# A delta-rule attention and feed-forward kernel: halves of the inverse by pairs, turns in transpose mode, one more block by quarters, and an opening written out step by step

## The chip, the core and the metric

The kernel runs on one core of one Trainium2 chip. A core has a matrix engine (PE), whose weight loads (PEld) overlap its matmuls, a vector engine (DVE), a scalar engine (ACT), a third engine for simple work on SBUF (POOL), and an engine (SP) that here only issues transfers. Each runs its own list of instructions strictly in order, and they wait for each other through semaphores. PE writes to PSUM, and DVE or ACT must copy the result from there to SBUF before PE can use it again. The metric is the device time of one execution in microseconds (us), median of several; less is better.

## What is computed

```python
k_n = k / (norm(k, axis=-1) + 1e-6)
state = zeros(B, H, D, D)                       # B=4, H=8, S=768, D=48
for t in range(S):
    y[t]  = q[t] @ state
    v_old = k_n[t] @ state
    state = state + beta[t] * outer(k_n[t], v[t] - v_old)
x = y.transpose(0, 2, 1, 3).reshape(B * S, H * D)          # 3072 x 384
h = x @ w_in                                               # 384 x 2048
out = maximum(0.01 * h, h) @ w_out                         # 2048 x 384
```

All of it is in float32.

## The kernel before

**Tiling.** The 768 steps are cut into 12 blocks `n` of 64. Inside a block the recurrence becomes matrix algebra: the triangular matrix made of the products of keys and of `beta` has to be inverted for each of the 32 heads and sequences, and the state is then carried from block to block. The 32 are cut into two groups `g` of 16. The feed-forward part treats the 256 rows of a block in 16 units `f`: `first` (L522) makes 9 matmuls into `ph`, ACT and DVE split the result into a high and a low part (`gh`, `gl`), and `second` (L537) makes 6 matmuls into `po`. Products that have to be exact are thus made of three products of such parts; the small ones of the attention use plain float32, which shows as two records per matmul.

**The steps of a block.** A letter stands for each, with the block and group it works on:

- `Q` loads k and q, `G` (gram, L173) multiplies them into `pg`, and ACT copies the part for the inverse to `gs`; `O` (L194) writes it to DRAM as `gd`, `I` (L225) reads it back as `L` with one matrix per partition; `R` (L203) masks the other part for later use; `M` (L217) copies corners that the halves need.
- `e` advances the inverse on DVE by one step (`inverse`, L294): norms, set-up, then one elimination per column. Blocks 0 and 1 are inverted together, by quarters of 16 rows: 15 eliminations give the diagonal blocks of 16 x 16. Every other block takes 31 eliminations on halves of 32 x 32.
- `D` (L327) writes the inverse to DRAM as `td`, `t`/`T` (L339) a turned copy as `tt`, and `A` (L352) reads both back, heads on the free axis, into `rt` and `gm`.
- For blocks 0 and 1, `P`, `H`, `J` (`halves_a`, `_b`, `_c`, L370 to L404) join quarters to halves on PE: `P` turns one quarter and multiplies the corner by another, `H` multiplies the two, `J` turns the result. One product is made per head and half: 64, 32 and 16 matmuls per group. For later blocks `C` (L406) moves the copy that came through DRAM.
- `Z` and `U` (L414, L426) join the two halves; `F`, `N` bring the norms, `V` scales v; `K`, `W`, `S`, `Y` (L470 to L504) are the products with keys, values, state and queries; `X` (`columns`, L506) turns y into `x` by a matmul with the identity, one per 128 columns and group, and splits it into `xh` and `xl`.
- `B` loads k, v and q of a block for these products; `c` loads beta.

The weights arrive as raw words (`l`, L115), and `w` takes them through 7 steps of conversion on ACT and DVE in turn (`convert`, L119), 16 tiles of 768 KB. Until block 0's units are done these conversions run beside them.

**What sets the order.** The program is emitted in a written order, and every engine keeps it. `PROLOGUE` is a text of such letters that ends with `X@0`; then for each block and unit a small plan (`PLAN` for blocks 0 to 3, `STEADY` for the rest) names what is emitted before and after the unit's `first` and `second`. `second` runs two units behind. A step is emitted whole: its matmuls and, right behind them, the copies that ACT or DVE make of the result. While block n is in the feed-forward part, the attention of block n+1 and the inverse of n+2 are interleaved with it. Transfers are issued from SP, and the first ones also from ACT (`kq` of blocks 0 and 1, the first two weight tiles). Four PSUM banks rotate among the small products.

## Time and profile before

| | us |
|---|---|
| median of 3 runs (lowest, highest) | 680.76 (677.38, 685.29) |
| the profiled execution's own time | 679.8 |
| its span | 678.0 |
| busy: PE, DVE, ACT, POOL | 614.3, 443.0, 350.9, 6.5 |
| bytes moved, mean rate | 60.48 MB, 89 GB/s |
| ph, 1728 matmuls, first one at | 76.2 |

The page gives busy times of engines, slices of the span, the chain of work that ended last, and groups of equal instructions. A row of the chain reads: start, length, engine (or "issue", where the engine waited for nothing that the profile shows), output tile, source line and number of records. A row of a group reads: line, engine, operation, output<-inputs, shapes, count, then busy us, mean ns of one, idle time before it and what ended that.

### The profile page before, as it was taken

What the parts mean: (1) busy time and instruction counts of PE and PEld (TensorE: products, weight loads), DVE (VectorE), ACT (ScalarE), POOL (GpSimd) and SP (SyncE); (2) the same over time, 40 slices, a digit from 0 to 9 for tenths busy, and PEclk for the clock granted to TensorE, in tenths of its full rate; (3) what the DMA queues carried; (4) which work ended last, traced back from release to release, by engine and by line L of the source; (5) the groups of instructions that cost most, each with busy time, mean ns of one, the idle gap of its engine ahead of it and who ended that gap; (6) DMA issues with size and microseconds to landing.
All of it is one profiled execution on the core that took longest, in us unless ns stands there. A gap on an engine that the chain in (4) does not pass through costs nothing.

```text
span 678.0 us, 22510 instructions
## 1 busy us (share of the span) xinstructions
PE 614.3 (91%) x9192; PEld 582.7 (86%) x9192; DVE 443.0 (65%) x1957; ACT 350.9 (52%) x875; POOL 6.5 (1%) x12
## 2 busy tenths in 40 slices
PE   4026878999999998999999999999999999999997
PEld 3025767989898898999999999999999999999996
DVE  4895759688868766777667578578577676621221
ACT  3544647734654654646556545555545546465432
POOL 3000000000000000000000000000000000000000
PEclk9999968999999999999999999999999999999999
DMA  8884562343235235247056064154353360340001
GB/s 207 202 266 165 117 207 48 77 82 63 65 82 100 57 86 104 51 88 148 3 110 128 7 133 99 43 102 94 70 90 80 80 104 10 72 71 3 16 10 23
DMA packets 126279, 60.48 MB, mean 89 GB/s; under 512 B 112992, under 2 KB 116192, under 8 KB 126176
## 3 DMA queue, kind: packets, MB, share of 16 engines
q1 hardware_dynamic: 125488, 56.57, 38.5%
q10 hardware_dynamic: 688, 2.48, 1.3%
q8 instruction: 72, 1.18, 0.7%
q14 instruction: 31, 0.25, 0.1%
HBM read 46.70 MB, written 12.32 MB: 87 GB/s over the span
## 4 chain that ended last, share of the span: by engine, by line
PE 74%; DVE 11%; DMA 6%; issue 3%; ACT 2%; SPq 2%; ACTq 0%; DVEq 0%
PE ph L528 28%; PE po L545 24%; PE pk L474 3%; PE py L502 3%; PE pw L482 3%; PE pg L188 2%; PE pc L492 2%; PE px L513 2%; PE pu L432 2%; PE pz L422 2%; DMA kq<-in_kqT 2%; DVE tmp L266 2%; DVE T L271 1%; DMA wr<-in_w_all 1%; DMA L<-gd 1%
## 5 line engine op out<-in xcount | busy, mean ns | idle before, releaser
L528 PE MATMUL ph<-xh,w 128*128 128x256 f32 x1152 | 248.0, 291 | 3.0 <-DVE gl L534 2.9
L528 PEld LDWEIGHTS ph<-xh,w 128*128 128x128 f32 x1152 | 192.6, 191 | 11.9 <-DVE gl L534 5.2
L534 DVE TENSOR_TENSOR gl<-ph,gh 128x256 fp32r<-128x256 f32 x192 | 81.2, 423 | 183.3 <-ACT ph L533 181.5
L545 PE MATMUL po<-w,gh 128*128 128x384 f32 x768 | 198.4, 340 | 0.3 <-ACT ob L551 0.3
L528 PE MATMUL ph<-xl,w 128*128 128x256 f32 x576 | 163.2, 283 | 0.0
L532 ACT ACTIVATE gh<-ph 128x256 fp32r<-128x256 f32 x192 | 74.0, 385 | 159.4 <-PE ph L528 144.4
L545 PEld LDWEIGHTS po<-w,gh 128*128 128x128 f32 x768 | 129.9, 190 | 0.5 <-ACT ob L551 0.5
L545 PE MATMUL po<-w,gl 128*128 128x384 f32 x384 | 130.0, 339 | 0.0
L528 PEld LDWEIGHTS ph<-xl,w 128*128 128x128 f32 x576 | 110.1, 191 | 0.0
L271 DVE TENSOR_TENSOR T<-T,tmp 128x60 f32<-128x60 f32 (+4 forms) x600 | 98.3, 204 | 0.7
L266 DVE TENSOR_TENSOR tmp<-T,L 128x60 f32<-128x60 f32 (+4 forms) x600 | 97.6, 203 | 0.4
L533 ACT ACTIVATE ph<-ph 128x256 f32<-128x256 f32 x192 | 72.8, 379 | 0.0
L545 PEld LDWEIGHTS po<-w,gl 128*128 128x128 f32 x384 | 72.8, 190 | 0.0
L210 DVE TENSOR_TENSOR rq<-pg,csb 64x256 f32<-64x256 f32 x92 | 38.9, 423 | 7.5 <-ACT gs L192 5.8
L188 PE MATMUL pg<-kq 48*64 48x128 f32 x736 | 28.8, 295 | 7.4 <-DMA kq<-in_kqT 7.3
L476 ACT ACTIVATE rt<-pk 48x512 f32<-48x512 f32 x44 | 26.1, 593 | 16.9 <-PE pk L474 16.1
L188 PEld LDWEIGHTS pg<-kq 48*64 48x64 f32 x736 | 22.5, 144 | 12.2 <-DMA kq<-in_kqT 6.6
L484 ACT COPY rv<-pw 64x384 f32<-64x384 f32 x46 | 21.8, 473 | 14.8 <-PE pw L482 13.9
L482 PEld LDWEIGHTS pw<-rv,rt 128*64 128x64 f32 x768 | 24.6, 143 | 2.8 <-ACT gh L532 2.5
L192 ACT COPY gs<-pg 128x256 f32<-128x256 f32 x46 | 15.0, 382 | 22.9 <-PE pg L188 22.9
L474 PEld LDWEIGHTS pk<-rt,rk 64*48 64x48 f32 x704 | 22.0, 126 | 5.1 <-ACT ph L533 2.8
L502 PEld LDWEIGHTS py<-rv,rq 128*64 128x64 f32 x768 | 23.7, 138 | 2.9 <-ACT ph L533 2.5
(80 smaller groups left out, 616.1 us busy)
## 6 DMA issues: line engine op xcount, KB each, us to landing
wr<-in_w_all SPq DMA_DIRECT2D x14, 768.0 KB, 10.0
kq<-in_kqT SPq DMA_DIRECT2D x44, 192.0 KB, 4.4
L<-gd SPq DMA_DIRECT2D x22, 256.0 KB, 3.8
rk<-in_kv SPq DMA_DIRECT2D x24, 192.0 KB, 4.1
rv<-in_kv SPq DMA_DIRECT2D x24, 192.0 KB, 4.4
rq<-in_qT SPq DMA_DIRECT2D x24, 192.0 KB, 4.7
out<-ob SPq DMA_DIRECT2D x48, 96.0 KB, 2.2
gd<-gs SPq DMA_DIRECT2D x96, 32.0 KB, 1.7
```

What stands on the lines that cost most here:

```text
L188: nc.tensor.matmul(pt[b][c * 64:(c + 1) * 64, p * 128:(p + 1) * 128], kq[r, c ^ b, p, 0], kq[r, c ^ b, p].rearrange("p x t -> p (x t)"), s ...
L210: nc.vector.tensor_tensor(qa[DN, c, b * NPAIR:(b + 1) * NPAIR], pv[b][r, 1], tri[r].rearrange("p (o t) -> p o t", o=1).broadcast_to([C, NP ...
L266: nc.vector.tensor_tensor(tv, t[:, :, j:j + 1].broadcast_to([P, k, w]), L[:, j, j + 1:].rearrange("p (o w) -> p o w", o=1).broadcast_to([P ...
L271: nc.vector.tensor_tensor(t, t, tv, ALU.subtract)
L474: nc.tensor.matmul(pv[r, u], k[DN, c, u], t[DN, c, u], start=True, stop=True)
L482: nc.tensor.matmul(pv[r, u], t[:, c, u], v[:, c, u], start=True, stop=True)
L502: nc.tensor.matmul(pv[s * C:(s + 1) * C, u * D:(u + 1) * D], qa[:, c, u], v[:, c, u], start=True, stop=True)
L528: nc.tensor.matmul(ph, a[f][:, cc * P:(cc + 1) * P], xs[n][cc][e], start=(k == 0), stop=(k == 3 * NCC - 1))
L532: nc.scalar.activation(gh, ph, AF.Prelu, alpha=0.01)
L533: nc.scalar.activation(ph, ph, AF.Prelu, alpha=0.01)
L534: nc.vector.tensor_tensor(gl, ph, gh.bitcast(F32), ALU.subtract)
L545: nc.tensor.matmul(po[t][:, :DO], a[:, ts_], w[f], start=(f == 0 and k == 0), stop=(f == NFC - 1 and k == 2))
```

## The change

It has five parts.

1. **Halves by pairs.** `P`, `H` and `J` work on the whole 64 x 64 diagonal block of a head. `P` makes 16 products of a corner tile that holds zeros outside the corners (`corners`, cleared by POOL), and 8 turns of two heads each in transpose mode; `H` makes 16 products on the diagonal blocks; `J` makes 8 turns of two heads each. ACT and DVE share the copies.
2. **x turned in transpose mode.** `X` uses the transpose instruction in place of a matmul with the identity.
3. **Block 2 by quarters.** With `QUARTERS = 3`, block 2 is inverted in 15 eliminations on quarters, with the lower and upper quarter on different partitions, and goes through `P`, `H`, `J`; its turned copy no longer goes through DRAM.
4. **The opening.** `PROLOGUE` and the plans of the first five blocks give way to one text, `OPENING`, of 1065 steps, in which `a`, `h`, `g`, `b` are the parts of a unit (first product, ACT's part, DVE's part, second product). A step is emitted without its copies, which stand later in the text under their own names with `a` (ACT), `v` (DVE) or `s` (store) behind. From block 5 on `STEADY` holds as before.
5. **Queues.** The first two weight loads go to SP, and the four `gd` writes of block 1's second group to ACT; `B1@0`, `B0@0` and `c@3` are issued earlier; a `rt` tile of blocks 1 and 2 is cleared by POOL before it is read into.

```diff
     def load_w(f):
-        (nc.scalar if f < 2 else nc.sync).dma_start(raw[:, 1:1 + 8 * DO], w_all[:, f].rearrange("p x n -> p (x n)").bitcast(U16))
+        nc.sync.dma_start(raw[:, 1:1 + 8 * DO], w_all[:, f].rearrange("p x n -> p (x n)").bitcast(U16))
...
     def gram_out(n, g):
-        gs = gss[n, g]
+        gs, q = gss[n, g], nc.scalar if n == g == 1 else nc.sync
...
     def inverse(b):
+        quarter = not two and NB[b][0] < QUARTERS
...
-        for j in range((HQ if two else HC) - 1):
-            if two:
+        for j in range((HQ if two or quarter else HC) - 1):
+            if quarter:
+                eliminate(b, L, j, T, j + 1)
+            elif two:
                 eliminate4(L4, j, T4)
...
     def load_t(n, g):
         T, Tt = Tts[n]
         t, gl = of("t", n, g), slice(g * GH, (g + 1) * GH)
+        if 0 < n < QUARTERS:
+            nc.gpsimd.memset(t[R0:R0 + HC, :, :, HC:] if n == 1 else t[R0:P], 0.0)
+        if 2 <= n < QUARTERS:
+            for e in (1, 0):
+                for x in range(2):
+                    a, d = R0 + e * HC + x * HQ, slice(x * HQ, (x + 1) * HQ)
+                    nc.sync.dma_start(t[a:a + HQ].rearrange("p h u i -> p (h u) i")[:, :, e * HC + x * HQ:e * HC + (x + 1) * HQ],
+                                      T[e, d, gl, d])
+            return
...
     def halves_a(n, g):
         t, w = of("t", n, g), nm.pop((n, g))
-        for l, h, u in lu:
-            for e, a, r in quad:
-                nc.tensor.matmul(pq[a:a + HC, 0, l], t[r, h, u, a:a + HC], eye[r, r.start:r.start + HQ], start=True, stop=True)
-        for l, h, u in lu:
-            for e, a, r in quad:
-                nc.tensor.matmul(pq[a:a + HQ, 1, l], w[r, l], t[r, h, u, a + HQ:a + HC], start=True, stop=True)
+        for p, j, h, u, r in pairs:
+            nc.tensor.matmul(pc[r, p], w[R0:P, h, u].rearrange("p e t -> p (e t)"),
+                             t[R0:P, h, u].rearrange("p (e t) -> p e t", e=2)[:, :, HQ:], start=True, stop=True)
+        for p in range(GU):
+            nc.tensor.transpose(pa[:, p], t[R0:P, p // 4, p % 4 * 2:p % 4 * 2 + 2].rearrange("p u t -> p (u t)"), eye[R0:P, R0:P])
...
+        later("a", lambda: move(nc.scalar.copy, pc, "gh", FB))
+        later("v", lambda: move(nc.vector.tensor_copy, pa, "yt", YT_BUFS))
...
     def halves_c(n, g):
-        for l, h, u in lu:
-            nc.tensor.matmul(tv[:, l], t[R0:R0 + HC, h, u, 0:HC], eye[R0:R0 + HC, R0:R0 + HC], start=True, stop=True)
+        for q in range(GU):
+            nc.tensor.transpose(tv[:, q], t[R0:R0 + HC, q // 4, q % 4 * 2:q % 4 * 2 + 2].rearrange("p u t -> p (u t)"),
+                                eye[R0:R0 + HC, R0:R0 + HC])
...
     def columns(n):
-                nc.tensor.matmul(x[:, g * P:(g + 1) * P], ys[n, g][:, cc * P:(cc + 1) * P], eye, start=True, stop=True)
+                nc.tensor.transpose(x[:, g * P:(g + 1) * P], ys[n, g][:, cc * P:(cc + 1) * P], eye)
...
     statics()
-    for text in PROLOGUE:
...
-    for n in range(nblk):
+    corners(0)
+    play(0, OPENING, False)
+    for n in range(CUT, nblk):
...
+CUT = 5
+OPENING = (
+    "c@0 Q@0 Q@1 s c@3 l@0 l@1 B1@0 G0@0 G1@0 R0@0 G0@0a M0@0 O0@0 R0@0v G1@0a R1@0 G0@1 M1@0 G1@1 G0@1a R0@1 w@0 m@1 O1@0 R1@1 G1@1a M0@1 R1@1v w@0 R0@1v "
+    "w@1 R1@0v O1@1 w@1 O0@1 M1@1 w@0 I@0 w@0 w@1 B0@0 w@1 I@1 w@1 l@2 l@3 w@0 l@4 w@1 l@5 w@1 w@0 w@0 e@0 w@2 e@0 F@0 N@0 N@1 N@0a e@0 N@1a w@3 e@0 e@0 "
...
+    "w@7 W1@0 W0@0a w@7 W1@0a A1@1 w@7 W1@0v W0@0v Y1@0 w@8 w@9 w@7 Y0@0 Y1@0a w@6 S0@0 Y0@0a w@9 S0@0a X@0 B0@1 S1@0 X@0a X@0a X@0v X@0a X@0v w@6 X@0v "
+    "G0@2 w@6 S1@0a B1@1 a R0@2 w@8 h P1@1 w@8 G0@2a a g l@14 P1@1a P1@1v O0@2 w@9 b h w@8 w@8 H1@1 g R0@2v b w@9 H1@1a w@10 a w@8 w@11 H1@1v V1@1 G1@2 h "
...
+    "e@6 a h g g b e@6 D@6 a h g b a h g b a h g b b h g "
+)
```

More of the change, by code (lines that the diff above doesn't have):

```diff
@@ L49 @@
 R0 = 64
+QUARTERS = 3
 @with_exitstack
@@ L160, in delta_moe_kernel, with later, shared @@
     betas, Xs, kqs, pgs, gss, gds, Lh, gm, nm, nrm, invs, Tts, nts, zss, ys, xs = ({} for _ in range(16))
+    late, rest = [], {}
+    def later(lane, fn):
+        late.append((lane, fn))
+    def shared(two, scalar, vector):
+        if two:
+            later("a", lambda: scalar(0))
+            later("v", lambda: vector(1))
+        else:
+            later("a", lambda: scalar(0, 1))
     def ps(x, n, g):
@@ L463, in values, with scale @@
         v = of("v", n, g)
-        for s in range(GS):
+        def scale(s):
             us = slice(s * NPAIR, (s + 1) * NPAIR)
@@ L474, in step_k, with move @@
             nc.tensor.matmul(pv[r, u], k[DN, c, u], t[DN, c, u], start=True, stop=True)
-        for c in range(2):
-            nc.scalar.mul(t[UP, c], pv[c * 64:c * 64 + D], -1.0)
+        def move():
+            for c in range(2):
+                nc.scalar.mul(t[UP, c], pv[c * 64:c * 64 + D], -1.0)
+        later("a", move)
     def step_w(n, g):
@@ L482, in step_w, with move @@
             nc.tensor.matmul(pv[r, u], t[:, c, u], v[:, c, u], start=True, stop=True)
-        for c in range(2):
-            (nc.vector.tensor_copy if n == 0 and c else nc.scalar.copy)(v[DN, c], pv[c * 64:c * 64 + C])
+        def move(copy, *cs):
+            for c in cs:
+                copy(v[DN, c], pv[c * 64:c * 64 + C])
+        shared(n == 0, lambda *cs: move(nc.scalar.copy, *cs), lambda *cs: move(nc.vector.tensor_copy, *cs))
     def step_s(n, g):
@@ L492, in step_s, with move @@
             nc.tensor.matmul(pv[r, u], k[:, c, u], v[:, c, u], start=True, stop=True)
-        for c in range(2):
-            nc.scalar.copy(v1[UP, c], pv[c * 64:c * 64 + D])
+        def move():
+            for c in range(2):
+                nc.scalar.copy(v1[UP, c], pv[c * 64:c * 64 + D])
+        later("a", move)
     def step_y(n, g):
@@ L555, in second, with ffn_next, first @@
                     nc.sync.dma_start(out[r0:r0 + C], obs[a:a + C, t])
+        later("s", store)
+    def ffn_next(x):
+        n, f = next(ffn[x], (None, None))
+        if n is not None:
+            dict(a=ffn_a, h=ffn_h, g=ffn_g, b=ffn_b)[x](n, f)
+        return n, f
+    def first():
+        for x in "ahg":
+            ffn_next(x)
+    def second():
+        n, f = ffn_next("b")
+        if f == NFC - 1:
+            operate(("o", n), results, (n,))
     def inv_steps(b, k):
@@ L569, in delta_moe_kernel, with operate, play @@
     once = {
-        "Q": (3, loads_kq), "I": (3, gram_in), "D": (2, bounce), "N": (1, turn_norms), "X": (1, columns),
-        "F": (1, lambda n: scales(where[n][0])), "d": (1, bounce), "T": (2, bounce_turned), "t": (1, bounce_turned), "i": (2, gram_in), "c": (3, load_beta)}
-    def play(n, text):
-        for name, g, at, k in re.findall(r"([A-Za-z])([01]?)(?:@(\d+))?(?:\*(\d+))?", text):
+        "o": (0, results), "Q": (3, loads_kq), "I": (3, gram_in), "D": (2, bounce), "N": (1, turn_norms), "X": (1, columns),
+        "F": (1, scales_of), "d": (1, bounce), "T": (2, bounce_turned), "t": (1, bounce_turned), "i": (2, gram_in), "c": (3, load_beta)}
+    def operate(key, fn, args, lane=None):
+        if lane:
+            rest[key, lane].pop(0)()
+            return
+        late.clear()
+        fn(*args)
+        for x, f in late:
+            if lane is None:
+                f()
+            else:
+                rest.setdefault((key, x), []).append(f)
+    def play(n, text, whole=True):
+        for name, g, at, k, lane in re.findall(r"([A-Za-z])([01]?)(?:@(\d+))?(?:\*(\d+))?([avs]?)", text):
             if name in "ef":
@@ L580, in play @@
                     inv_steps(where[m][0], int(k or 1))
+            elif name == "w" and at:
+                f = int(at)
+                if f not in conv:
+                    conv[f] = convert(f)
+                next(conv[f])
             elif name == "w":
```

228 lines of the change are left out of this document (133 added, 95 removed), and 32 rows, old and new, of tables (OPENING, PLAN).

## The prediction, made before the changed kernel was run

> **What bounds the kernel now.** I read four views in turn: the page's first part, the busy times of four stretches cut at the first matmul of the feed-forward part (ph), at block 1's and at block 5's first ph, then the chain of work in those stretches, then groups by line.
>
> ```profile
> PE 614.3 (91%) x9192; PEld 582.7 (86%) x9192; DVE 443.0 (65%) x1957; ACT 350.9 (52%) x875; POOL 6.5 (1%) x12
> 0.00:76.16 76.16, 31.83 (x911) 29.27 (x911) 54.92 (x151) 34.42 (x68) 6.53 (x12) 1.00 0.68 191
> 76.16:152.14 75.98, 65.43 (x1206) 60.93 (x1203) 56.92 (x144) 43.76 (x94) 0.00 (x0) 0.84 0.45 114
> 152.14:352.51 200.37, 196.51 (x2809) 184.44 (x2809) 147.80 (x764) 105.77 (x276) 0.00 (x0) 1.00 0.40 80
> 352.51:678.00 325.49, 320.54 (x4273) 308.03 (x4272) 183.40 (x902) 166.96 (x438) 0.00 (x0) 1.00 0.33 66
> ```
>
> Columns of a stretch: length, busy PE, PE's loads, DVE, ACT, POOL, granted clock, DMA share, GB/s. The start takes 76.16 us and block 0 another 75.98, at a clock of 0.84. From block 1 on PE is busy 98% of the time, so only less PE work helps there; in the first 152 us it isn't the bound. The steady chain gives PE's prices:
>
> ```profile
> 352.68 1.08 PE ph L528 x9
> 353.75 1.04 PE po L545 x6
> 365.60 1.13 PE pz L422 x64
> 366.73 1.26 PE ph L528 x9
> 369.04 1.13 PE pu L432 x64
> 374.58 1.92 PE pk L474 x64
> 378.83 2.00 PE pw L482 x64
> 385.27 2.00 PE py L502 x64
> 387.27 1.44 PE pc L492 x64
> 391.02 1.34 PE px L513 x12
> 392.36 1.03 PE pg L188 x32
> ```
>
> A unit (first and second product of one f) is 1.08 + 1.04 = 2.12 us, and a ph right behind a small product takes 1.26, so each such switch costs 0.2. The attention of one block is 1.13 + 1.13 + 1.92 + 2.00 + 2.00 + 1.44 + 1.34 + two pg of 1.03 = 13.0.
>
> The early chain shows what PE lost:
>
> ```profile
> 6.35 9.73 DMA wr<-in_w_all
> 16.10 0.30 SPq L199
> 21.78 3.73 DMA L<-gd
> 38.24 1.97 DVE rv L466 x4
> 45.27 1.89 PE pq L377 x64
> 50.09 2.77 issue
> 55.44 3.62 issue
> 77.48 1.12 PE pq L377 x64
> 80.46 2.77 issue
> 84.21 2.22 PE ph L528 x9
> 87.34 4.00 issue
> 92.83 2.22 PE ph L528 x9
> ```
>
> A ph that takes 2.22 instead of 1.08 is PE at half its clock, behind the idle stretches; the pq at 45.27, 1.89 against 1.12, tells the same of the start. The four pieces of "issue" are PE waiting for its own instructions:
>
> ```profile
> 0.00:50.09 50.09, 13.30 (x350) 11.81 (x350) 38.29 (x124) 21.71 (x44) 6.53 (x12) 1.00 0.84 222
> 0.00:55.44 55.44, 15.57 (x478) 13.75 (x478) 42.20 (x130) 24.14 (x48) 6.53 (x12) 1.00 0.86 241
> 0.00:80.46 80.46, 36.13 (x1114) 33.33 (x1114) 58.27 (x157) 38.68 (x76) 6.53 (x12) 1.00 0.69 192
> 0.00:87.34 87.34, 40.24 (x1242) 37.07 (x1242) 62.44 (x164) 40.65 (x81) 6.53 (x12) 0.98 0.71 192
> q8 instruction: 72, 1.18, 0.7%
> ```
>
> They come after 700, 956, 2228 and 2484 PE instructions (matmuls plus loads), in each pair 256 apart, and 1.18 MB in 72 packets is 16 KB, or 256 of the 18384 instructions at 64 bytes, a packet. Where PE uses 256 small instructions faster than the next packet comes, it stands for 2.8 to 4.0 us.
>
> **The change, part by part.**
>
> *x turned in transpose mode.* The px of a block are 6 products of two records, 1.34 us for 12, or 0.112 each. A transpose should be one record with the same weights, so 6 x 0.112 = 0.67: 0.67 saved. Bounds: nothing (1.34, a turn priced as a product) and 1.0 (0.34, if the single pass also halves the spacing); I take 0.67, since a ph record with the same 128 columns of weights also keeps 1.08 / 9 = 0.12. Six px lie behind block 5's start, on a PE that is never idle: 4.0 us (0 to 6). Four more lie in blocks 1 to 4, 2.7, and one in block 0.
>
> By the Trainium skill, "TensorE: Matmul & The Clock Gate", Terms, transpose mode is four times faster for FP32; by it px would be 0.34, and six would save 6.0 instead of 4.0. No row here shows a transpose.
>
> *Halves by pairs.* A group had 64 + 32 + 16 = 112 products, each two loads and two matmuls: 448 instructions. It gets 16 products and 8 turns (P), 16 products (H) and 8 turns (J): 32 x 4 + 16 x 2 = 160. PE's time hardly changes: before, 224 matmul records a group at 1.12 / 64 (pq at 77.48) are 3.9 at most; after, 16 products like pw (2.00 / 32 = 0.0625) are 1.0, 8 turns at 0.06 to 0.11 another 0.5 to 0.9, H 1.0, J 0.5, together 3.2. I count nothing for it. What goes is the burst: a block's 320 instructions instead of 896. I take all four "issue" pieces as gone, 13.2 us of PE's idle time. What is late next is DVE, so not all of it comes off the end. Block 2 joins, at 6.4 us of PE.
>
> *Block 2 by quarters.* DVE's rows:
>
> ```profile
> L534 DVE TENSOR_TENSOR gl<-ph,gh 128x256 fp32r<-128x256 f32 x192 | 81.2, 423 | 183.3 <-ACT ph L533 181.5
> L271 DVE TENSOR_TENSOR T<-T,tmp 128x60 f32<-128x60 f32 (+4 forms) x600 | 98.3, 204 | 0.7
> L266 DVE TENSOR_TENSOR tmp<-T,L 128x60 f32<-128x60 f32 (+4 forms) x600 | 97.6, 203 | 0.4
> L129 DVE TENSOR_SCALAR ca<-ca 128x768 bf16<-128x768 bf16 x16 | 5.7, 357 | 3.4 <-ACT ca L127 3.3
> L135 DVE SCALAR_TENSOR_TENSOR cg<-wr,cg 128x768 uint32<-128x768 uint32 x16 | 15.3, 958 | 3.1 <-ACT cg L133 3.0
> L137 DVE SCALAR_TENSOR_TENSOR cg<-wr,cg 128x768 uint16<-128x768 uint16 x16 | 16.4, 1028 | 0.1
> L144 DVE TENSOR_TENSOR w<-cg,w 128x768 fp32r<-128x768 f32 x16 | 15.3, 953 | 0.9 <-ACT w L142 0.9
> ```
>
> An inverse of one block is (98.3 + 97.6) / 10 = 19.6 us of steps; 15 steps on quarters cost at most what the pair of blocks 0 and 1 takes (from the landing of L, 21.78 + 3.73 = 25.51, to the rv at 38.24 it is 12.7 with norms and set-up, some 7.5 of it steps). So DVE is given back 12 us, and the bounce of the turned T goes; its price is the PE time above and twice the DMA issues (4 and 8) on SP.
>
> *Loads on other queues.* The gd write at 16.10 waited for a weight load issued at 6.35: in program order it is the eighth transfer behind it, so a transfer is issued only when the eighth before it has landed. The change puts kv and q of block 0 (B1) ahead of the gd writes and three more (B0) between the two reads of L. Each is 192 KB like a kq. In return the weight loads leave ACT's queue, and four gd writes go there, in front of ACT's copies. I take L 1.5 us later (from 2 earlier to 3 later): 27.
>
> *The start.* T is done 12.7 later, 39.7; bounce and reload take 45.27 - 38.24 = 7.0 and one more issue, so P starts at 47 (before: 45.27). From T's end to the first ph, DVE's list holds 26 conversion steps (6 to 8 of each row above, 20.6) and 9.6 of scalings and copies: 30.2, less some 3 where a step starts under the one before; 67 if DVE never waits. PE, at half clock here, makes each of its P, H, J, Z, U, W, Y, X late by a copy each, some 5 us of DVE waiting. First ph at 72; bounds 67, and 78, where P to ph takes the 30.9 us of before.
>
> *Block 0.* PE: 16 units 33.9, P, H, J of blocks 1 and 2 12.8, the attention products in the list 12.1, 17 switches 3.4: 62. DVE: 16 gl of 0.42, 30 conversion steps 25.7, block 2's inverse 11.5, gram masks 4.7, the rest 14: 63, less 3 of overlap. 62 and 60, and tied together in order; I add a tenth: 68. Bounds 63, and 80, where DVE keeps the share of 56.92 / 75.98 = 0.75.
>
> *Blocks 1 to 4.* PE's list: 64 units 135.7, attention 52, 31 switches 6.2: 194. Before, 64 x 2.12 + 4 x 13.0 + 28 switches x 0.2 = 193 took 200.37, a loss of 7; I take 4, since part of that was block 1 catching up: 198 (194 to 205). The order splits groups into single steps, but the switches per block don't grow.
>
> *The clears by POOL* cost nothing on the path: POOL is busy 6.5 us in all, and the tiles are cleared a group ahead; without that cover it would be about a microsecond per load.
>
> Sum: 72 + 68 + 198 + 325.5 - 4.0 = 659.5 of span. The profiled run has 679.8 around a span of 678.0, so 661.3; the median of the runs shown, 680.76, lies 1.0 above that: 662.
>
> **The rivals.**
>
> 1. *All covers hold.* Start 67, block 0 63, blocks 1 to 4 194, the rest 319.5 with px at 0.34: 643.5 and the 2.8 around the span make 646. For it: in-order lists that alternate single steps. Against: it needs PE at 62 of 63 and DVE at 60.
>
> 2. *Nothing gained in the opening.* The start ends at 76 again (L later, DVE loaded) and DVE keeps its 0.75, so block 0 takes 80: 76 + 80 + 198 + 321.5 + 2.8 = 678. For it: DVE has 60 us of work there where it did 56.92 in 75.98. Against: part of that share was PE standing for instructions.
>
> 3. *The change doesn't do what it says for px:* a turn costs a product. Then 4.0, 2.7 and 0.7 don't come: 669. By the Trainium skill, "TensorEngine Tiling (Array Packing)", Restrictions, column tiling disables transpose mode for FP32 input; px and the turns of P fill all 128 columns, those of J only 64, so by that rule only J would lose, about half a microsecond per group. No run here shows it yet.
>
> 4. *The clock, the case that ends slower.* Block 0 has PE waiting for DVE in many short gaps. If those keep it at half clock, the ph of 2.22, throughout, its 62 us become 124 and the time 718. Before, a mean of 0.84 is 24 us at half clock. Slower by 1% begins at 688, with block 0 at 94, which is half clock for 52 us of it. For it: the gaps that set it off were 2.77 and 4.00 us. Against: those very gaps go, and the list never leaves PE without work for long. The Trainium skill, "TensorE: Matmul & The Clock Gate", Part 4, says that transposes don't count as PE activity for the clock; by it 32 turns per block would add to such gaps. The trace has none to judge by.
>
> **How the numbers follow.** The forecast, 662, has a chance of 0.54, with its own range of 651 to 673; rival 1 0.17, rival 2 0.14, rival 3 0.08, rival 4 0.07. A measurement of this kernel can tell about 1% from no change: 674 and 688 are the bounds. Faster: 0.54 + 0.17 + 0.08 = 0.79; within 1%: rival 2, 0.14; slower: 0.07. A range of 647 to 679 leaves out rival 4, half of rival 1 and a little of rival 2, 0.19.
>
> **What would show it.** Right: first ph near 72; no "issue" of 2 us or more on PE before block 1; clock above 0.9 in block 0; block 1's first ph near 140; block 5's near 338; px 6 records in 0.67, and each block behind shorter by as much. Wrong: L landing past 30, ph of 2.22 for most of block 0, px at 1.34, or PE idle behind ACT's copies in blocks 1 to 4, where single steps now follow each other with little between.

## The result, and the profile after

| | us |
|---|---|
| before, median of 14 runs (lowest, highest) | 679.88 (676.35, 685.29) |
| after, median of 14 runs (lowest, highest) | 686.96 (682.57, 691.71) |
| ratio of after to before, 95% interval | 1.0102 (1.007 to 1.0133) |
| the profiled execution after, its span | 686.91, 685.1 |

The change made the kernel 1% slower; 662 was forecast. Ratios here and below leave out executions that the chip disturbed; where a median stands beside one, it doesn't.

The first part of the page of the kernel after, and its busy times in the four stretches of the prediction (start, block 0, blocks 1 to 4, the rest), cut at the same first ph; columns as before:

```profile
PE 627.1 (92%) x8704; PEld 592.2 (86%) x8704; DVE 439.7 (64%) x1905; ACT 355.3 (52%) x892; POOL 15.9 (2%) x22
```

```profile
0.00:79.69 79.69, 35.11 (x650) 32.45 (x650) 59.18 (x156) 39.39 (x79) 12.11 (x18) 1.00 0.74 219
79.69:148.27 68.58, 66.58 (x1013) 61.14 (x1010) 58.19 (x162) 46.50 (x106) 3.75 (x4) 0.93 0.35 77
148.27:361.40 213.13, 207.83 (x2811) 195.24 (x2810) 140.76 (x702) 102.99 (x270) 0.00 (x0) 0.94 0.39 77
361.40:685.10 323.70, 317.54 (x4237) 303.33 (x4235) 181.62 (x888) 166.43 (x438) 0.00 (x0) 1.00 0.32 63
```

| stretch | before | predicted | after |
|---|---|---|---|
| start | 76.16 | 72 | 79.69 |
| block 0 | 75.98 | 68 | 68.58 |
| blocks 1 to 4 | 200.37 | 198 | 213.13 |
| the rest | 325.49 | 321.5 | 323.70 |

The span is 25.6 us over the 659.5 of the prediction's sum: 15.1 in blocks 1 to 4, 7.7 in the start, 2.2 in the rest and 0.6 in block 0, which is where it was forecast. In blocks 1 to 4 PE has as many records as before, 2811 against 2809, but is busy for 207.83 us with them against 196.51, at a granted clock of 0.94 against 1.00, and idle for only 5.3. So most of what is lost there isn't idle time: PE is slow. The next rows are the same view of the kernel after, cut at the four stretches in which the clock was half, each behind the 3.4 us ahead of it (the clock is the first number behind the five engines):

```profile
106.10:109.50 3.40, 1.40 (x24) 0.93 (x23) 3.20 (x13) 0.56 (x2) 0.00 (x0) 1.00 0.00 0
109.50:119.70 10.20, 10.20 (x137) 9.33 (x133) 7.29 (x33) 5.28 (x11) 0.00 (x0) 0.50 0.01 2
167.50:170.90 3.40, 1.28 (x8) 0.97 (x8) 3.04 (x12) 1.07 (x4) 0.00 (x0) 1.00 0.45 98
170.90:174.30 3.40, 3.40 (x15) 3.21 (x14) 3.20 (x15) 0.66 (x2) 0.00 (x0) 0.51 0.02 5
215.30:218.70 3.40, 2.79 (x91) 2.43 (x86) 3.40 (x28) 3.26 (x10) 0.00 (x0) 1.00 0.49 121
218.70:232.30 13.60, 13.60 (x127) 12.80 (x122) 7.00 (x51) 4.61 (x11) 0.00 (x0) 0.50 0.01 1
307.50:310.90 3.40, 2.21 (x41) 1.85 (x39) 0.95 (x3) 1.87 (x5) 0.00 (x0) 1.00 0.16 25
310.90:321.10 10.20, 10.20 (x119) 9.19 (x118) 1.24 (x5) 3.97 (x8) 0.00 (x0) 0.50 0.26 59
```

Half clock comes here in multiples of 3.4 us: 10.2, 3.4, 13.6 and 10.2. The first two falls follow stretches in which PE stood most of the time (busy 1.40 and 1.28 of 3.40 us), as I had assumed. Before the fourth it was busy 2.21. Before the third it was busy 2.79, 1.5 of it with pz and pu, and the clock fell all the same and stayed down for 13.6 us in which PE never stood. Of the 27.2 us at half clock in blocks 1 to 4, half, 13.6, is lost; 207.83 less 13.6 is 194.2, the 194 that the prediction had for PE's list.

The chain there, and ahead of the second fall, at the start of block 3's inverse, where PE stood for DVE:

```profile
162.63 4.41 DMA L<-gd
167.06 0.20 DVE sr L276
...
170.17 0.43 DVE gl L633
170.64 1.42 PE ph L622 x6
...
217.94 1.39 PE pu L500 x62
219.34 2.22 PE ph L622 x9
221.55 1.88 PE pk L549 x32
```

ph takes 2.22 in place of 1.08, and 32 records of pk 1.88 where the steady loop has 64 in 1.92. The upper rows are the other loss: DVE, in order, stood for block 3's L before it could make the gl that PE waited for.

The start: SP's issue of the second reading of L, and DVE's first step behind its landing, from the timelines of the kernel after (start, length, engine, line, operation, tiles; in brackets the idle time before and what ended it):

```profile
26.48 0.45 SPq L257 DMA_DIRECT2D L<-gd  x1
```

```profile
29.78 0.19 DVE L276 TENSOR_SCALAR sr<-L 128x32 uint32<-128x32 uint32 x1 [0.47 <-DMA L<-gd]
```

From the end of T, the inverse (42.39), to P, and from P to the first ph, by the stretches view:

```profile
42.39:49.44 7.05, 0.00 (x1) 0.03 (x1) 6.97 (x13) 4.16 (x6) 0.00 (x0) 1.00 0.78 120
49.44:79.69 30.25, 27.02 (x518) 25.08 (x518) 20.92 (x35) 19.08 (x37) 1.03 (x2) 1.00 0.76 260
```

L, which landed at 25.51 before, lands by 29.78. In the last row PE is busy 27.02 of 30.25 us, and for the most part slowly, since pe's 32 records take 1.92 here and 1.05 at full clock (in b5_start, below). (The recorded clock of 1.00 in this stretch is not to be trusted: the records' lengths show half, and profiles of other runs below do record 0.50 there.)

### The profile page after: what moved, and what is told of

Same layout as the page of the kernel before. It is cut to its first block, busy times and chain, and to the rows that moved or that the text cites. A ratio compares the mean times of both kernels' runs of the same rounds, so it can differ in the third digit from the quotient of the medians.

```text
span 685.1 us, 21522 instructions
## 1 busy us (share of the span) xinstructions
PE 627.1 (92%) x8704; PEld 592.2 (86%) x8704; DVE 439.7 (64%) x1905; ACT 355.3 (52%) x892; POOL 15.9 (2%) x22
## 4 chain that ended last, share of the span: by engine, by line
PE 65%; DVE 5%; DMA 3%; SPq 2%; ACT 2%; issue 1%; ACTq 0%; DVEq 0%
PE ph L622 26%; PE po L643 24%; PE pw L560 3%; PE pk L549 3%; PE py L586 3%; PE pg L199 2%; PE pc L573 2%; DVE rq L226 2%; DMA L<-gd 1%; PE pu L500 1%; PE pz L484 1%; PE px L600 1%; DVE gl L633 1%; DMA gd<-gs 1%; DMA gm<-tt 1%
## 5 line engine op out<-in xcount | busy, mean ns | idle before, releaser
L622 PEld LDWEIGHTS ph<-xh,w 128*128 128x128 f32 x1152 | 194.1, 192 | 11.5 <-DVE gl L633 6.3
L643 PE MATMUL po<-w,gh 128*128 128x384 f32 x768 | 201.9, 344 | 0.2 <-ACT ob L651 0.2
L303 DVE TENSOR_TENSOR T<-T,tmp 128x60 f32<-128x60 f32 (+16 forms) x569 | 92.4, 202 | 0.7
L298 DVE TENSOR_TENSOR tmp<-T,L 128x60 f32<-128x60 f32 (+16 forms) x569 | 92.0, 202 | 0.6
L560 PEld LDWEIGHTS pw<-rv,rt 128*64 128x64 f32 x768 | 27.4, 156 | 3.2 <-ACT gh L628 1.5
L586 PEld LDWEIGHTS py<-rv,rq 128*64 128x64 f32 x768 | 25.9, 145 | 4.9 <-ACT rv L564 1.9
L586 PE MATMUL py<-rv,rq 128*64 128x48 f32 x768 | 28.2, 231 | 1.4 <-ACT rv L564 1.3
L560 PE MATMUL pw<-rv,rt 128*64 128x48 f32 x768 | 29.2, 241 | 0.0
```

The costliest lines, as they stand in the source:

```text
L298: nc.vector.tensor_tensor(tv, t[:, :, j:j + 1].broadcast_to([P, k, w]), L[:, j, j + 1:].rearrange("p (o w) -> p o w", o=1).broadcast_to([P ...
L303: nc.vector.tensor_tensor(t, t, tv, ALU.subtract)
L560: nc.tensor.matmul(pv[r, u], t[:, c, u], v[:, c, u], start=True, stop=True)
L586: nc.tensor.matmul(pv[s * C:(s + 1) * C, u * D:(u + 1) * D], qa[:, c, u], v[:, c, u], start=True, stop=True)
L622: nc.tensor.matmul(ph, a[f][:, cc * P:(cc + 1) * P], xs[n][cc][e], start=(k == 0), stop=(k == 3 * NCC - 1))
L643: nc.tensor.matmul(po[t][:, :DO], a[:, ts_], w[f], start=(f == 0 and k == 0), stop=(f == NFC - 1 and k == 2))
```

## The experiments

First the parts of the change one by one, then the clock, then the start. Ratios are to the kernel before, each with its 95% interval.

| kernel | ratio |
|---|---|
| after | 1.0102 (1.007 to 1.0133) |
| p1_px: before, px by transposes | 0.9997 (0.9977 to 1.0017) |
| p2_halves: before, halves by pairs | 0.9889 (0.9853 to 0.9926) |
| a1_px_product: after, px by products | 1.0101 (1.0064 to 1.0138) |
| a2_transfers: after, old order of transfers | 1.0056 (1.0026 to 1.0085) |
| a9_order: after, gram copies ahead of DVE's reading | 1.0058 (1.003 to 1.0087) |
| a3_fill: after, fill of 128 x 128 | 0.9971 (0.9946 to 0.9997) |
| a3_small: after, fill of 128 x 16 | 0.9975 (0.9952 to 0.9999) |
| r1_spread: as b2_both, steps moved in place of fill | 0.9956 (0.9927 to 0.9986) |
| b1_fill: p2_halves, px by transposes, small fill in block 0 | 0.9893 (0.9857 to 0.9929) |
| b2_both: after, both old orders, small fill | 0.9892 (0.9869 to 0.9914) |
| a4_warm: after, fill from T's end to Y | 1.0151 (1.0096 to 1.0206) |
| a8_warm: after, fill where PE stands | 1.0185 (1.0157 to 1.0213) |
| b3_start: b2_both, start filled | 0.99 (0.9868 to 0.9933) |
| b4_start: the same, P too | 0.9886 (0.9823 to 0.9948) |
| b5_start: the same, gap before P too | 0.9907 (0.9882 to 0.9932) |

### px by transposes, alone and undone

```diff
-                nc.tensor.matmul(x[:, g * P:(g + 1) * P], ys[n, g][:, cc * P:(cc + 1) * P], eye, start=True, stop=True)
+                nc.tensor.transpose(x[:, g * P:(g + 1) * P], ys[n, g][:, cc * P:(cc + 1) * P], eye)
```

> The kernel before with the px turns alone, 6 transposes a block in place of 6 products; no other line is touched. My theory now: a turn costs half of a product (6 records in 0.66 to 0.67), but from block 5 on DVE's gl at the block's end comes last, so a block of 48.47 loses only 0.1 to 0.2, and the whole kernel 2 to 3 us: 677 to 678. Rival, the step of my prediction: all of it is on PE's path, 12 blocks times 0.67, 8 us: 672. Third: a turn costs a product, px stays at 1.34 and the time at 680.

> The kernel after with px by products again, all else as it is. Theory (DVE's gl ends the steady block): px at 1.34 again, the steady block 48.33 grows by 0.1 to 0.2, the whole by 1 to 3 us: 688 to 690. Rival (all on PE's path): 12 times 0.67, 8 us: 695. If px were what makes the kernel after slow, it would fall below 687.

Alone in the kernel before it does nothing that can be told (678.92 against 679.56), and undone in the kernel after it changes nothing that can be told either (1.0101 against 1.0102). The price was right: in the chain of the kernel after a block's px stands as

```profile
273.89 0.66 PE px L600 x6
```

0.66 in place of 1.34. But from block 5 on, a block (from its first ph to the next one's) only goes from 48.47 to 48.33. The chain at the end of block 5 says why:

```profile
403.88 1.10 PE pg L199 x32
404.98 0.36 ACT gs L207
405.38 0.42 DVE gl L633
...
408.79 0.29 DVE gm L233
409.11 0.44 DVE gl L633
409.59 1.34 PE ph L622 x9
```

Between 405.38 and 409.55 the chain is DVE's alone: a gl, two steps of the inverse, four rq, two gm, a gl, and only then PE's ph. PE comes there half a microsecond sooner and waits for it. Only in blocks 9 and 10, which have less of this work, does nearly the whole saving come (45.99 to 45.43 and 44.55 to 43.88), so the rest gains 1.8 in place of 4.0.

### Halves by pairs, alone

The functions of the kernel after with `QUARTERS = 2` and px by products, run in the order of the kernel before (`PROLOGUE` and `PLAN`, its own queues):

```diff
-QUARTERS = 3
+QUARTERS = 2
...
-    play(0, OPENING, False)
+    for text in PROLOGUE:
...
-        1: "P|w"
+        1: "P l@14 l@15|w"
```

> The kernel before, in its own order and with its own transfers, block 2 by columns and px by products as before; only the halves of blocks 0 and 1 go by pairs of heads (160 PE instructions a group in place of 448), with the cleared corner tiles that this needs. Theory: the four pieces of issue of 2.77 to 4.00 us vanish, and with them most of block 0's idle time and half of its half clock; first ph at 71 to 74 in place of 76.2, block 0 at 66 to 70 in place of 76, the whole 666 to 672. Rival: what is late next (copies of ACT and DVE in series between the small products) takes the place of the issue pieces; first ph 75 to 76, block 0 73 to 76, the whole 675 to 680.

672.34: of all parts this is the one that gains. Its first ph comes at 72.5 (before 76.2), and no "issue" of 2 us or more is left on PE, as predicted. Block 0 still takes 75.5; what is late next there are copies, and half clock:

```profile
72.50:148.00 75.50, 69.27 (x917) 64.14 (x916) 56.31 (x145) 44.61 (x98) 0.00 (x0) 0.80 0.45 114
```

### The order of the first transfers and of the gram copies

`a2_transfers` puts the queues back and `B1@0`, `B0@0` behind the second reading of L; `a9_order` leaves the transfers and lets ACT copy a gram before DVE reads the same PSUM tile:

```diff
-"... l@0 l@1 B1@0 G0@0 ... I@0 w@0 w@1 B0@0 w@1 I@1 ..."
+"... l@0 l@1 G0@0 ... I@0 w@0 w@1 w@1 I@1 B1@0 B0@0 ..."          (a2_transfers)
-"... G1@0 R0@0 G0@0a ... R1@1 G1@1a ..."
+"... G1@0 G0@0a R0@0 ... G1@1a R1@1 ..."                          (a9_order)
```

> The kernel after with the transfers of the start in the order of the kernel before: kv and q of block 0 behind the second read of L in place of ahead of the gd writes and between the two reads of L, the first two weight loads on ACT's queue, all gd writes on SP's. Theory: L lands at 25.5 to 26.5 in place of 29.75, T's end and P come as much earlier, first ph at 76 in place of 79.7, and all behind it moves with it: 683. Rival (from T's end on, the chain of DVE's conversion steps and copies sets the first ph): L earlier, first ph within 1 us of 79.7, 686 to 687.

> The kernel after, with ACT's copy of a gram emitted ahead of DVE's reading of the same PSUM tiles for block 0's first and block 1's second group; transfers and all else as in the kernel after. Theory (the two readers of one tile run one behind the other, so the order sets when gd can be written): L lands 1.5 to 2.5 sooner than 29.75, and all behind it: 684 to 686. Rival (L waits for the transfers in front of its reading, not for the copy): L within 0.5 of 29.75, 686 to 688.

DVE's first step behind L, in the timelines of a2_transfers, a9_order and b2_both (which has both edits):

```profile
27.30 0.18 DVE L276 TENSOR_SCALAR sr<-L 128x32 uint32<-128x32 uint32 x1
```

```profile
30.00 0.19 DVE L276 TENSOR_SCALAR sr<-L 128x32 uint32<-128x32 uint32 x1 [0.41 <-DMA L<-gd]
```

```profile
24.96 0.18 DVE L285 TENSOR_SCALAR sr<-L 128x32 uint32<-128x32 uint32 x1
```

The transfers alone give 2.5 us back (29.78 to 27.30), the copies alone nothing (30.00), both together 4.8. In the kernel after, SP stood 4.3 us for the `gd` writes before it could issue the second reading of L at 26.48; ACT issued the last four of them from 19.29 on, and in a9_order, where the copies were done sooner, still from 19.56 on. So the transfers stand in front of the copies' turn: only with them out of the way does it show that ACT's copy waits behind DVE's reading of the same tile. The first ph follows: 79.7, 77.3 and 75.0 in after, a2_transfers and b2_both. By the ratios alone neither stands clear of the kernel after, since the intervals touch; the profiles tell them apart. a9_order's L is no sooner, so what its ratio shows isn't a gain by way of L. Its profile has 20.5 us of half clock in place of 37.5, but it is that of its fastest execution (676.52, the others 682.32 to 688.71), so where the ratio comes from stays open.

### What lowers the clock

Three kernels put work that nobody reads into six blocks of the kernel before, one kind per block; each was executed once. The rows of a product are here those of its weights, the partitions over which it sums.

```diff
+            if f == 3 and n in PROBE:
+                fill(n, *PROBE[n])
...
+    def fill(n, k, m, times):
+        p = ps("pd", n, 0)
+        for _ in range(times):
+            nc.tensor.matmul(p[0:m, 0:P], eye[0:k, 0:m], eye[0:k], start=True, stop=True)
```

> The kernel before with 36 products of 128 columns each, one behind the other and read by nobody, behind the second product of f = 1 in blocks 5 to 10; the output is untouched. They take the same columns and the same time at full clock (8.0 us, 0.223 each by the px row) and differ only in how much of TensorE's 128 x 128 array they use: 32 rows x 32 columns in block 5, 128 x 128 in block 6, 64 x 64 in block 7, 128 x 64 in block 8, 128 x 48 in block 9, 128 x 40 in block 10. Theory: the clock follows the share of the array in use over some 3.4 us, not whether PE is busy: it falls to half inside the probes of block 5 (share 0.06) and 7 (0.25), with ph or probe records at twice their length behind, and holds in block 6 (1.0) and 8 (0.5); between 0.32 and 0.38, blocks 9 and 10, it may go either way. Rival, the reading behind my prediction (idle stretches lower the clock): PE is busy in all six, so the clock stays full in all six.

> As the first probe (36 products of 128 columns in each of blocks 5 to 10 of the kernel before), with other weights: 32 rows x 128 columns in block 5, 128 x 32 in block 6, 32 x 64 in block 7, 64 x 32 in block 8, 64 x 128 in block 9, 128 x 16 in block 10. In the first probe only 32 x 32 lowered the clock; 64 x 64 with a quarter of the array did not. Theory now: the share of the array's rows in use counts. The clock falls in blocks 5 and 7 (32 of 128 rows) and holds in 6, 8, 9 and 10. Rival, columns count: it falls in blocks 6, 8 and 10 and holds in 5. Rival, rows times columns: it holds in 5 and 6 (0.25, as 64 x 64 did) and falls in 7, 8 and 10 (0.125).

> The kernel before with filling work behind the second product of f = 1, read by nobody: 72 transposes of 128 x 128 in block 5, 72 transposes of 64 rows x 128 columns in block 6, 72 products of 64 rows x 64 columns that alternate between two halves of the columns in block 7, 144 of 32 rows x 32 columns that alternate in the same way in block 8 (as pz does), and for comparison 18 full products in block 9 and 36 of 128 rows x 64 columns in block 10. Theory (rows in use count, transposes as any other work): the clock falls in block 8 alone. Rival (transposes don't count as work for the clock): it falls in blocks 5, 6 and 8, inside the 8 us of transposes.

The stretches of the probes, by the same view. c1_probe, blocks 5 and 7 (32 x 32, 64 x 64); c2_probe, blocks 5, 7, 8 and 10 (32 x 128, 32 x 64, 64 x 32, 128 x 16); c3_probe, blocks 5 and 8 (transposes of 128 x 128; alternating 32 x 32):

```profile
360.50:372.90 12.40, 12.40 (x74) 10.28 (x73) 3.80 (x13) 0.00 (x0) 0.00 (x0) 0.63 0.57 119
...
480.10:488.20 8.10, 8.10 (x74) 7.93 (x73) 3.80 (x13) 0.00 (x0) 0.00 (x0) 1.00 0.74 168
```

```profile
364.10:376.20 12.10, 12.10 (x74) 11.88 (x73) 3.77 (x13) 0.00 (x0) 0.00 (x0) 0.66 0.65 127
...
484.00:496.20 12.20, 12.20 (x74) 11.87 (x73) 3.75 (x13) 0.00 (x0) 0.00 (x0) 0.65 0.53 118
547.10:555.10 8.00, 8.00 (x74) 7.65 (x73) 3.77 (x13) 0.00 (x0) 0.00 (x0) 1.00 0.79 170
...
658.10:666.20 8.10, 8.10 (x74) 7.00 (x73) 0.20 (x1) 0.00 (x0) 0.00 (x0) 1.00 0.36 71
```

```profile
360.10:368.10 8.00, 8.00 (x75) 8.00 (x74) 3.87 (x13) 0.00 (x0) 0.00 (x0) 1.00 0.80 172
...
522.80:534.90 12.10, 12.10 (x290) 11.93 (x289) 3.75 (x13) 0.00 (x0) 0.00 (x0) 0.66 0.62 123
```

PE is busy throughout in every row. The clock falls in the four probes whose weights have 32 rows, whatever their columns, and in none of the fourteen with 64 or 128 rows, not even with 16 columns, and not in transposes. So idle time isn't the only cause, and my first theory, the share of the array's area, falls; of the readings that were forecast, rows in use is the one that fits the probes. (In c3_probe the two probes of 64 rows lasted only 4.7 and 4.4 us and say less.)

pz and pu are products of 32 rows, but rows alone don't give the rule for the kernels. Two stretches of 3.4 us speak against it. In p2_halves the clock fell at 77.0, behind pe and pq of block 1, with PE busy throughout and no product of fewer than 64 rows; pe's products there are only 32 columns long, those of the probes of 64 rows that kept the clock for 8 us are 128. And at 304.1 the kernel after kept its clock with pz and pu for 2.2 of 3.4 us:

```profile
73.61:77.02 3.41, 3.41 (x82) 3.16 (x80) 2.40 (x5) 3.37 (x7) 0.00 (x0) 1.00 0.69 186
77.02:87.27 10.25, 9.63 (x92) 9.22 (x91) 7.21 (x11) 5.83 (x16) 0.00 (x0) 0.50 1.03 246
```

```profile
304.06:307.48 3.42, 3.42 (x161) 3.17 (x156) 1.72 (x5) 2.64 (x8) 0.00 (x0) 1.00 0.02 5
```

Idle time alone isn't the rule either: in the kernel before PE was busy only 2.44 of the 3.41 us from 219.91, with products of 128 rows, and the clock stayed at 1.00, while 2.79 of 3.40 with pz and pu among them didn't hold it. How rows, the length of the products and idle time add up within one piece of 3.4 us was not measured.

The Trainium skill, "TensorE: Matmul & The Clock Gate", Part 1, says that the clock follows how busy PE was in free-running windows of about 3.4 us; the pieces of 3.4 us agree, the busy 32-row probes at 0.63 to 0.66 don't. The Trainium skill, "TensorE: Matmul & The Clock Gate", Part 4, says that transposes don't count as PE work for the clock in the same way; the probe at 360.10, 8 us of them at 1.00, disagrees.

### Holding the clock in the kernel after

```diff
-"... F@2 g Z0@1v b w@12 ..."        (block 0)
+"... F@2 g Z0@1v y@7 b w@12 ..."
-"... g F@3 e@3 b h a e@3 ..."       (block 1)
+"... g F@3 e@3 b h y@8 a e@3 ..."
-"... N@4 Z0@3 ... U0@3 h U1@3 ..."  (block 2)
+"... N@4 x@3 Z0@3 ... x@3 U0@3 h x@2 U1@3 ..."
...
```

`x@k` puts k filling products into the PSUM tile of the next small product, ahead of it; `y@k` into one of its own; 8 more stand ahead of U and K of block 4. The block numbers in the two expectations below are those of the attention steps.

> The kernel after with 31 products of 128 x 128 x 128 more on PE, read by nobody: 7 and 8 in the two stretches where PE stands for gl (at 105.98 and 168.19), 3 + 3 + 2 ahead of pz and the two pu of block 3, 2 + 2 + 4 ahead of the pu and pk of block 4; 6.9 us of work at full clock, some 4 of it in stretches where PE stands anyway. Theory (share of the array in use sets the clock): the half clock at 109.5 to 119.7, 170.9 to 174.4, 218.7 to 232.4 and 310.9 to 321.1 (37.5 us, 18.8 lost) goes for the most part, and the kernel with more work is faster: 672 to 679. Rival (busy or idle sets it, or the half clock is not on the path): the fill costs what it is, 688 to 691.

> As the run before it, with the same 31 extra products at the same places and of the same columns, but with weights of 128 rows x 16 columns in place of 128 x 128. Theory: an eighth of the array is too little to hold the clock; the four stretches of half clock stay, and the time is that of the kernel after or 1 to 3 us more: 687 to 690. Rival (idle time of PE is what lowers the clock, and any work prevents it): as fast as the run before it.

Both are 9 us faster than the kernel after, though PE does 31 products more. The fill also takes up time in which PE stood, so these runs don't tell rows from idle time. My expectation for the small fill (an eighth of the array is too little) was wrong in the way that the second probe then explained: it has 128 rows. In a3_small's profile block 0 has a clock of 1.00, blocks 1 to 4 have 0.98:

```profile
80.40:145.10 64.70, 64.31 (x1028) 58.40 (x1025) 58.10 (x162) 46.48 (x106) 3.76 (x4) 1.00 0.37 81
145.10:352.50 207.40, 204.24 (x2847) 190.12 (x2847) 140.66 (x701) 102.43 (x268) 0.00 (x0) 0.98 0.39 80
```

Block 0 is 3.9 shorter than in the kernel after. Blocks 1 to 4 are 5.7 shorter; what is left there over the 198 of the prediction is 5.1 of half clock that remained at 301.7 (10.2 us) and some 5 of filling. In b2_both, which has the same fill and is described below, the clock holds throughout blocks 1 to 4:

```profile
139.70:345.50 205.80, 201.85 (x2859) 188.02 (x2858) 141.25 (x702) 103.18 (x270) 0.00 (x0) 1.00 0.40 80
```

Whether an order without fill among the small products does the same (`r1_spread`):

```diff
-"... x@3 U0@3 h x@2 U1@3 e@4 U0@3a a g ... Z1@5a g G1@6 ... O1@6 a U0@5a ..."
+"... U0@3 h e@4 U0@3a a U1@3 g ... Z1@5a g a G1@6 ... O1@6 U0@5a ..."
```

> The kernel with transfers and copies in the old order and the small fill (671.7), with the 16 filling products among the small products of blocks 3 and 4 taken out again and three steps moved in their place: a ph between the two pu of block 3's attention ahead of both pk, and a ph moved ahead of pg of block 6 between pz and pu of block 5; the 15 in the two stretches where PE stood for gl stay. Theory (products of 32 rows side by side let the clock fall, feed-forward products between them hold it): no half clock in blocks 2 to 4, and the 3.6 us of filling come off: 667 to 670. Rival: the clock falls again in one or two of these places, 10 us of half clock each: 673 to 678.

It doesn't. The chain of r1_spread ahead of pk of block 5:

```profile
296.73 0.44 DVE rq L235
297.24 0.37 ACT gs L216
...
298.42 0.38 ACT rt L514
298.85 0.38 PE pk L558 x2
```

The ph that was moved ahead had hidden this: pk waits for ACT's copy of pu (rt), which stands behind ACT's copy of pg (gs), which stands behind DVE's last reading of the same pg (rq); PE stands for 2.36 us. The clock falls there for 10.2 us, and at 210.2, where pu now waits 1.25 us for a copy of pz, for 6.8; in b2_both it held in both places. Since PE stood ahead of both falls, this run doesn't show that ph between the small products would hold the clock.

### The start

`b2_both` joins the two old orders with the small fill, `b1_fill` is p2_halves with px by transposes and fill in block 0 (26 products, not the 29 of its expectation).

> The kernel after with the transfers of the start as before, ACT's copy of the grams ahead of DVE's reading of the same PSUM tiles, and the small fill of 128 rows x 16 columns: the two edits that helped singly, together. Theory (they are independent: the start moves everything behind it, the fill keeps the clock): 683.6 less 8.7, 674 to 676. Rival: the shift moves the small products against the windows of the clock, and it falls somewhere else: 678 to 682.

> The kernel with the halves by pairs in the order of the kernel before (672.3), with px by transposes and 29 products of weights of 128 rows x 16 columns, 128 columns long, read by nobody, in block 0 alone: ahead of its pe, pv, pz, pu, pk and the pg of group 1, where PE stands for copies or for kq. Theory (too few rows in use let the clock fall in block 0, 30.7 us at half): most of the half clock there goes, block 0 at 64 to 69 in place of 75.5, the whole at 662 to 668. Rival (DVE, 56 us busy in block 0, and the copies set its length): block 0 at 73 to 76, the whole at 670 to 673.

b2_both gains more than the parts promised, since transfers and copies help only together. b1_fill brings block 0 from 75.5 to 71.8, less than expected:

```profile
71.10:142.90 71.80, 66.90 (x963) 60.38 (x961) 56.38 (x144) 44.97 (x100) 0.00 (x0) 0.93 0.49 120
```

The clock there is 0.93 in place of 0.80, and 3.7 us come of the 6.5 or more that were expected. What holds the rest was not tested; the rival named DVE's work and the copies. Both beat the kernels before and after, as does p2_halves.

From P to the first ph it still takes 30.8 us in b2_both. Five kernels fill the start to have the clock up by then: a4_warm and a8_warm on the kernel after, b3_start to b5_start on b2_both.

```diff
-"... N@0 N@1 N@0a ... P0@0 P0@0a ... H0@0 ... J0@0 ... Z0@0 ... U0@0 ..."
+"... N@0 N@1 y@40 N@0a ... x@10 P0@0 P0@0a ... x@4 H0@0 ... x@4 J0@0 ... x@3 Z0@0 ... x@3 U0@0 ..."   (b5_start)
```

> The kernel after with 24 products of 128 x 128 x 128 on PE between the end of the first inverse (42.4) and P (49.4), where PE stands idle, and 2 ahead of each of 12 of the small products from P to Y of block 0; read by nobody. Theory: PE at half clock is what sets the 30.3 us from P to the first ph; with the clock up at P, pe takes 0.96 to 1.1 in place of 1.92, pv 1.9 in place of 3.62, and the first ph comes 5 to 10 us sooner, at 70 to 75, the whole at 677 to 682. Rival (DVE's conversion steps and the copies in series set it): first ph at 78 to 80 with the clock up, the whole 686 to 688. Third: so few full products don't raise the clock at all, and the first ph comes 3 to 5 us later.

> The kernel after with products of 128 x 128 x 128, read by nobody, only where PE stands: 66 from the end of the first weight conversion on (from about 29), 6 at T's end, and 2 ahead of J, Z and U of each group but the first of J's. Theory (PE at half clock sets the time from P to the first ph): P stays within 0.5 of 49.4, pe takes 0.96 to 1.1 in place of 1.92 and pv 1.9 in place of 3.62, and the first ph comes at 70 to 75 in place of 79.7; the whole 677 to 682. Rival (DVE's list and the copies set it): with the clock up the first ph still comes at 77 to 80, the whole 684 to 688.

> The kernel with transfers and copies in the old order and the small fill (671.7, first ph at 75.0, P at 44.26), with 34 products of 128 rows x 16 columns behind N (from 33.8 on, where PE stands until P) and 1 to 4 ahead of H, J, Z, U, W and Y of block 0, so that 32-row products don't let the clock fall again. Theory (PE at half clock sets the 30.7 us from P to the first ph): P stays at 44.3, pe takes 0.96 to 1.1, pv 1.9, and the first ph comes at 66 to 71; the whole 663 to 668. Rival (DVE's list and the copies in series): with the clock up the first ph comes at 73.5 to 76 all the same, the whole 670 to 673. If PE's records stay at twice their length, the fill failed and the run says nothing.

> As the earlier fill of the start (the kernel with transfers and copies in the old order and the small fill; first ph at 75.0 without a fill of the start), with 37 filling products behind N, 2 and 3 ahead of the two P, and 3 to 4 ahead of H, J, Z and U; 30 of them, 6.8 us, stand between P and the first ph. Theory (half clock sets the 30.7 us from P to the first ph): with the clock up, the same work takes 16 us, the fill 6.8, some copies are waited for: first ph at 67 to 72, the whole at 663 to 669. Rival (DVE's list and the copies in series): the clock is up and the first ph still comes at 74 to 77, the whole at 671 to 674.

> The last fill of the start with 11 more filling products between N and P, so that PE doesn't stand for 1.95 us before P, and one more ahead of the second H. Theory (half clock sets the 30.7 us from P to the first ph): in an execution whose clock stays up, first ph 22 to 25 us behind P, at 67 to 71, and the whole at 664 to 669; in one whose clock falls, the fill costs twice its length and the first ph comes past 80. Rival (DVE's list and the copies in series): with the clock up the first ph still comes 29 to 31 us behind P, at 74 to 77, the whole at 671 to 674.

None gains. a4_warm's fill stands ahead of 11 small products. There the clock rose at 48.0 and fell again at 61.7, among pt and pz, so that the rest of the fill cost double. In a8_warm the fill stood in front of `N`, so that DVE's scalings came late, and the clock fell at 51.7. b3_start's profile has the clock down again at 48.0, inside P (its ten executions took 666.66 to 681.94; the best, with a recorded clock of 0.999 over the whole kernel, lies within what was expected of a clock that stays up, 663 to 668, but left no profile). b4_start's profile is that of its longest execution (681.20): PE stood 1.96 us before P in it, and the clock fell at 46.9. Only b5_start's profile has the clock up from P to W. The same steps in b2_both and in b5_start, by the stretches view, and some of b5_start's chain:

```profile
44.26:61.69 17.43, 15.43 (x289) 14.47 (x289) 13.09 (x23) 10.09 (x19) 0.00 (x0) 0.50 1.00 385
```

```profile
47.70:65.16 17.46, 17.46 (x372) 14.28 (x372) 11.17 (x21) 9.61 (x20) 0.00 (x0) 1.00 1.01 358
```

```profile
47.70 1.05 PE pe L441 x32
...
56.44 0.61 PE pt L473 x8
...
65.16 2.29 issue
```

At half clock PE needs 15.43 us for P, H, J, Z, U and waits 2.0; at full clock the steps take half (pe 1.05 against 1.92), the fill takes what that frees, and PE never waits. Right behind, PE stands 2.29 us for instructions, of which the fill is made as well: the stall comes after 1207 PE instructions, some two packets of 256 behind the 700 of the first stall in the kernel before. The clock falls at 66.5, and the first ph comes at 79.5. So PE's half clock accounts for 15.43 of these 17.43 us, but it isn't shown that it alone sets them: in b2_both the chain of work from 51.99 to 60.70 runs through copies and conversion steps of ACT and DVE. The fill of b5_start doesn't pay for itself. What would be left with the clock up and no fill isn't shown, but DVE's 13.09 busy microseconds of those 17.43 leave at most 4.3 to gain there.

## Why the prediction was wrong

**Loads, L.** Predicted 1.5 us later, measured at most 4.3 (25.51 to 29.78; the bounds were 2 sooner to 3 later). The new order of the transfers, which the prediction priced at these 1.5, gave 2.5 back when undone alone. One step was left out: DVE's `R` now stands ahead of ACT's copy of the same PSUM tile, and ACT's `gd` writes come behind that copy. Undoing both brought L's first use to 24.96, another 2.3 sooner; undoing this step alone brought nothing.

**The start.** From T's end to the first ph I had 27.2 of DVE's work and 5 of its waiting, from 39.7 to 72. Measured from 42.39: DVE busy 6.97 + 20.92 = 27.9, waiting 9.4. The list was right; the term that was mis-sized is the waiting, 9.4 for 5. Behind P, PE is busy 27.02 of the 30.25 us, for the most part at half clock; how much of the waiting that makes, and how much the copies in series, stays open. Of the 7.7 us over, 2.7 are L and T, 0.7 the list, 4.4 this waiting.

**Halves.** Right: the four pieces of issue are gone, P, H, J cost PE what was counted, and this part alone is worth 1.1%, some 7.5 us. Also right that not all 13.2 us come off the end.

**Block 2 by quarters.** The steps on DVE went from 98.3 + 97.6 to 92.4 + 92.0 us, 11.5 less for the 12 predicted. This part was not run by itself.

**Block 0.** 68.58 for 68, DVE 58.2 for 60, PE 66.58 for 62, of which 5.1 are half clock at 109.5. The size is right; a3_small's 64.7 at a clock of 1.00 suggests that the tenth I added was the clock, not the order.

**Blocks 1 to 4.** The step that failed: the sum takes PE's list of 194 at full clock and adds a loss of 4 for waiting, with no term for half clock there. PE's list was 194.2 at full clock, so the units, the attention and the switches were counted right, and its idle time was 5.3; the missing 13.6 is half clock. That it is the clock is shown: in b2_both, with the fill and a clock of 1.00 throughout, these blocks take 205.80 in place of 213.13, 24 filling products included. Rival 4 had the clock, but in block 0, by idle gaps alone, and with a chance of 0.07. Of the prediction's signs of being wrong only one shows, and faintly (PE waits 2.5 us for ACT in blocks 1 to 4); half clock there wasn't among them. Why it falls there is in part argued: the new order brings pz and pu of both groups close together and has PE stand for copies and for DVE, busy with the inverse; in the steady loop each small product stands between units of 128 rows on a PE that hardly stands. Which of the two decides at each fall was not separated.

**px.** The price was right (0.66 for 0.67; rival 3 falls, and for J as well: its eight turns take 0.61 at full clock). But J's turns have weights of 32 rows and 128 columns by the trace, not 64 columns as the prediction had it, so no run tests the rule on column tiling. That it all lies on PE's path was wrong: 1.8 of the 4.0.

**POOL's clears** cost nothing that shows: no wait of PE, DVE or ACT ends on them, and SP waited 0.4 us for one.

## What to carry to other kernels

A busy matrix engine can still be slow: where the granted clock of a stretch is below 1, compare one record's length with that of the same record in the steady loop before counting idle time. An order that gathers small products with few rows, or leaves PE standing beside them, can give back through the clock what it gains by overlap; filling products of 128 rows among them held the clock here and paid for themselves in blocks 0 to 4, while an order without such fill was not found. Count half clock as a term of its own when an order changes, also where PE is busy. A saving on one engine counts only if the chain at the end of the block still runs through that engine; here half a microsecond per block went from PE's work into PE's waiting.

## What the runs showed of the hardware

- The clock can fall on a busy engine: 8 us of products whose weights have 32 rows took 12.1 to 12.4 at a granted 0.63 to 0.66, with 32, 64 or 128 columns of weights; probes of 64 rows (128 columns long) and of 128 rows kept 1.00, the latter with as few as 16 columns of weights. 64 rows are not safe in themselves: in p2_halves 3.41 us of work without a gap, nearly all of it pe (64 rows, 32 columns long) and turns of 64 rows, were followed by 10.25 us at 0.50.
- Half clock can outlast what set it off. In the 13.6 us from 218.7 PE was busy throughout, with ph at 2.22 and pk at 1.88, and the clock came back only behind ph, po and ph in a row; in c1_probe a ph and a po behind the last product of 32 rows still took 2.22 and 1.92.
- A transpose of 128 x 128 takes half of a float32 product of the same size, 0.11 against 0.22, in this kernel.
- A filling product costs four PE instructions, and enough of them bring back the stalls for instructions: 2.29 us in b5_start.
- In this program the order in which two engines read one PSUM tile decides when the later one's transfer can start: 2.3 us of L in b2_both against a2_transfers. With the transfers of the kernel after in front of it, the same edit moved nothing (30.00 against 29.78).
